# Splitting a fused second MLP into an up phase and a seven-product down phase through DRAM

## The chip, the cores and the metric

The kernel runs on one core of a Trainium2 chip. The metric is the device time of one execution, in microseconds (us). Engines are named as the profile names them: PE (matmuls, with PEld its weight loads), ACT, DVE, POOL, and SP, which here only issues DMAs; POOL issues DMAs from a queue of its own.

## The reference

Three stages follow each other on 8 x 576 = 4608 tokens; everything is float32.

```python
attn: p_packed = sm_attn(p, k, v); x = sm_attn(q, p_packed, p_packed)   # 8 heads of 64, 32 packed queries
mlp 1: x = (silu(x @ w_gate) * (x @ w_val)) @ w_out                     # 512 -> 1536 -> 512
mlp 2: h = x @ w_in; g = h * cos(h); out = g @ w_out                    # 512 -> 2048 -> 512
```

## The kernel before

Every large product is taken in three passes over operands that are split into a high part, rounded for the matmul, and the low rest (`PASSES`): high x high, high x low, low x high. A split costs one ACT copy and one DVE subtraction over the operand (`split`, L103 to L105).

The attention and the up projections of the first MLP run block by block (8 blocks of 576 tokens, `a_up`), to some 430 us. Its down projection (`strassen`, L643 on, called from the loop over `SETS`: four sets of 1024 tokens and one of 512) uses a seven-product scheme: tokens and inner features are halved, the sums of the weight blocks were formed beforehand, those of the data are formed by DVE (`sums1`), each product accumulates in PSUM, and `evict` puts the results together. Its order is `ORDER`; after each product the next one's operands are split (`prep`), and later data is loaded (`load_h`). Results go to DRAM (`x2d`).

Weights arrive packed. `w2_step` does one step of a list (`w2_todo`): decode a block, form sums, split, store to DRAM for later. A pair of blocks takes 7 steps where the seven-product scheme needs it (`w2_pair`: `w1u`, `w2u`), and 2 per block where the weights are used as they are (`w2_put_d`: `w2d`). The steps are placed by hand: at the slots `STEPS` of the attention blocks 1 to 6, at four slots of block 7, and in the first three sets of the first MLP's down projection.

The second MLP runs from 690 us to the end, in one loop over 48 pairs `p` (L1040 on): 6 chunks of 768 tokens (two halves of `TH` = 384) by 8 pairs of feature blocks. Per pair, seven up products (`product`, L989) of six matmuls with 384 columns each go to four PSUM banks; ACT and DVE add them up and form h cos(h) in a four-deep pipeline of tiles of 128 x 384 (`slot`, called by `chain`), which ends with the split that the down projection needs. `step_down` puts down projections between the products: `down` (L1002) takes 128 tokens and four feature blocks, 12 matmuls of 512 columns, and the result is added into `oacc` in SBUF, from where whole rows of 2 KB are stored. Both sorts of weights are loaded again for each chunk, on SP's queue (`load_up`, `load_wd`); x is prepared for the next chunk in between (`load_x2`, `sums_x2`, `split_x2`). All order within an engine is the order of the program text (`manual_schedule`).

## Time and profile before

| what | value |
|---|---|
| median of 3 runs | 1442.2 us (1442.17 to 1444.04) |
| span of the profiled execution | 1440.2 us |
| attention and first up projections | to about 430 us |
| first MLP's down projection | about 430 to 690 us |
| second MLP | 690 us to the end |
| PE busy | 1427.2 us |

The span is the time from the first to the last instruction of one profiled execution; its own device time is not given beside it, so its span is compared with the median, and lies 2.0 us under it. In a profile row, a busy time is the sum over a group, "mean ns" the duration of one instruction, and what follows is the idle time of the engine just before the group's instructions, with what ended it. Instructions of one engine overlap by some tens of nanoseconds at their ends.

### The profile page before, as it was taken

How to read it: one execution, taken by the hardware profiler on the slowest of the kernel's cores; microseconds unless marked ns; L12 is line 12 of the kernel's file. 1: busy time of each engine (PE TensorE's matmuls, PEld its weight loads, DVE VectorE, ACT ScalarE, POOL GpSimd, SP SyncE). 2: the span in 40 equal slices, each digit the busy share in tenths (PEclk: the TensorE clock that was granted, in tenths of full speed). 3: DMA queues.
4: the chain of work that ended last, by engine and by line, in shares of the span. 5: the costliest groups of instructions: out<-in, count | busy, mean ns of one | idle time of the engine just before them, and what ended most of it. 6: DMA issues, size and time to landing. Idle time of an engine off the chain costs nothing.

```text
span 1440.2 us, 24944 instructions
## 1 busy us (share of the span) xinstructions
PE 1427.2 (99%) x9352; PEld 1252.1 (87%) x9352; DVE 1079.8 (75%) x1743; ACT 829.7 (58%) x1462; POOL 126.4 (9%) x232
## 2 busy tenths in 40 slices
PE   8999999999999999999999999999999999999998
PEld 6678888898998878898899999999999999999997
DVE  6769888988948799879867766866776776677564
ACT  5856656656735565554665655646656555555642
POOL 1112222222210111110000000000000000000000
PEclk9999999999999999999999999999999999999999
DMA  8947886795696756570985665685576668556641
GB/s 342 411 165 266 292 328 239 280 335 208 233 410 267 263 204 228 197 249 21 354 286 179 220 221 179 202 294 182 180 242 199 201 213 265 179 178 204 218 142 44
DMA packets 139352, 335.62 MB, mean 233 GB/s; under 512 B 15072, under 2 KB 25312, under 8 KB 137824
## 3 DMA queue, kind: packets, MB, share of 16 engines
q1 hardware_dynamic: 118272, 260.36, 53.5%
q0 software_dynamic: 20096, 71.84, 12.5%
q8 instruction: 74, 1.21, 0.3%
q10 hardware_dynamic: 864, 1.84, 0.3%
q14 instruction: 46, 0.38, 0.1%
HBM read 252.71 MB, written 81.26 MB: 232 GB/s over the span
## 4 chain that ended last, share of the span: by engine, by line
PE 94%; DVE 2%; ACT 1%; DMA 1%; issue 1%; POOL 0%; SPq 0%; ACTq 0%; DVEq 0%
PE acc L1009 27%; PE p L994 23%; PE o L655 16%; PE pg L538 10%; PE pv L538 10%; PE wp L498 3%; PE pv L527 2%; PE pg L527 1%; DMA hr<-h 1%; PE pp L227 1%; PE s L260 1%; PE tp L217 1%; PE s L180 0%; DVE hr L635 0%; DVE g L105 0%
## 5 line engine op out<-in xcount | busy, mean ns | idle before, releaser
L1009 PE MATMUL acc<-wd,g 128*128 128x512 f32 x1728 | 413.8, 389 | 0.0
L994 PE MATMUL p<-xs,up 128*128 128x384 f32 x2016 | 373.2, 337 | 2.9 <-issue 1.6
L1009 PEld LDWEIGHTS acc<-wd,g 128*128 128x128 f32 x1728 | 322.5, 188 | 57.1
L994 PEld LDWEIGHTS p<-xs,up 128*128 128x128 f32 x2016 | 353.7, 188 | 14.7 <-issue 1.9
L655 PE MATMUL o<-g,w 128*128 128x512 f32 (+1 forms) x1260 | 259.3, 368 | 1.0 <-DVE g L105 1.0
L655 PEld LDWEIGHTS o<-g,w 128*128 128x128 f32 x1260 | 219.2, 189 | 40.8 <-DVE g L105 1.7
L972 ACT ACTIVATE t<-c,quarter 128x384 f32<-128x384 f32 x144 | 88.4, 614 | 198.7 <-DVE c L1082 192.9
L538 PEld LDWEIGHTS pg<-a,wp 128*128 128x128 f32 x1008 | 137.8, 188 | 16.1 <-issue 8.2
L104 ACT ACTIVATE g<-hr 128x1024 fp32r<-128x1024 f32 (+1 forms) x105 | 101.5, 976 | 87.1 <-PE o L655 43.9
L538 PE MATMUL pg<-a,wp 128*128 128x288 f32 x1008 | 150.1, 298 | 0.0
L538 PE MATMUL pv<-a,wp 128*128 128x288 f32 x1008 | 150.1, 298 | 0.0
L538 PEld LDWEIGHTS pv<-a,wp 128*128 128x128 f32 x1008 | 137.6, 188 | 7.2 <-DVE h L570 3.3
L105 DVE TENSOR_TENSOR g<-hr,g 128x1024 fp32r<-128x1024 f32 (+1 forms) x105 | 113.4, 1114 | 34.7 <-ACT g L104 34.4
L556 ACT ACTIVATE silu<-pg 128x576 f32<-128x576 f32 x96 | 62.6, 652 | 116.1 <-PE pg L538 107.1
L570 DVE TENSOR_TENSOR h<-silu,pv 128x576 f32<-128x576 f32 x96 | 72.1, 752 | 60.4 <-PE pv L538 25.1
L1077 DVE TENSOR_TENSOR u<-v,p 128x384 f32<-128x384 f32 x48 | 26.6, 553 | 118.2 <-PE p L994 117.9
L982 DVE TENSOR_TENSOR g<-t,g 128x384 fp32r<-128x384 f32 x192 | 105.9, 552 | 8.0 <-ACT g L969 7.8
L974 DVE TENSOR_TENSOR t<-t,k 128x384 f32<-128x384 f32 x192 | 106.0, 552 | 3.5 <-ACT k L978 1.8
L975 ACT ACTIVATE t<-t 128x384 f32<-128x384 f32 x192 | 98.4, 513 | 2.7 <-DVE t L974 2.5
L969 ACT ACTIVATE g<-t 128x384 fp32r<-128x384 f32 x192 | 98.5, 513 | 0.4 <-DVE t L980 0.4
L978 ACT ACTIVATE k<-t 128x384 int32<-128x384 f32 x192 | 98.3, 512 | 0.0
L1023 DVE TENSOR_TENSOR oacc<-oacc,acc 128x512 f32<-128x512 f32 x108 | 73.8, 684 | 32.2 <-PE acc L1009 32.1
(108 smaller groups left out, 1428.7 us busy)
## 6 DMA issues: line engine op xcount, KB each, us to landing
up<-w2u SPq DMA_DIRECT2D x336, 256.0 KB, 3.2
wd<-w2d SPq DMA_DIRECT2D x96, 512.0 KB, 6.2
h<-h POOLq DMA_DIRECT2D x96, 288.0 KB, 4.9
hr<-h SPq DMA_DIRECT2D x48, 512.0 KB, 8.8
raw<-in_w SPq DMA_DIRECT2D x44, 512.0 KB, 4.4
w2u<-w2p POOLq DMA_DIRECT2D x24, 512.0 KB, 3.9
raw<-in_wgv SPq DMA_DIRECT2D x11, 1024.0 KB, 9.9
w<-w1u SPq DMA_DIRECT2D x21, 512.0 KB, 11.6
```

The source lines that it names most:

```text
L104: ACT.activation(out=hi, in_=src, func=AF.Copy)
L105: eng.tensor_tensor(out=lo, in0=src, in1=hi.bitcast(F32), op=ALU.subtract)
L538: PE.matmul(out=p_[:, c, :HS], lhsT=w[:, u, x, o:o + 128], rhs=a2[b][:, u, y, HS * c:HS * c + HS], start=(n == 0), stop=(n == 5),)
L655: PE.matmul(out=acc[:, m, :N], lhsT=wd1[n, fp][:, j, 256 * x + 128 * m:256 * x + 128 * m + 128], rhs=g1[n, fp][:, y, j, :], start=(first a ...
L969: ACT.activation(out=three["g"][:, 0, :], in_=three["t"], func=AF.Copy)
L972: ACT.activation(out=now["t"], in_=now["h"], func=AF.Identity, scale=1.0 / TWO_PI, bias=quarter)
L974: DVE.tensor_tensor(out=one_["t"], in0=one_["t"], in1=one_["k"], op=ALU.subtract)
L975: ACT.activation(out=one_["t"], in_=one_["t"], func=AF.Sin, scale=SIN_SCALE)
L978: ACT.activation(out=now["k"], in_=now["t"], func=AF.Copy)
L982: DVE.tensor_tensor(out=three["g"][:, 1, :], in0=three["t"], in1=three["g"][:, 0, :].bitcast(F32), op=ALU.subtract)
L994: PE.matmul(out=out, lhsT=w[:, u, 128 * k:128 * k + 128], rhs=x[:, v, k, :], start=(first and k == 0 and i == 0), stop=(last and k == 1 an ...
L1009: PE.matmul(out=acc, lhsT=gs[p, a, t][:, x, o:o + 128], rhs=wd[j, f][:, y, :], start=(f == 0 and n == 0), stop=(f == 3 and n == 2),)
```

## The change

The second MLP falls into two phases. In the **up phase** a loop over periods (`period`) works on three pairs at a time: the new pair's products 0, 1 and 2, the old pair's 3, 4, 6 and 5, and h cos(h) of the one before. Partial results are carried into the next product within PSUM: ACT copies one bank into another (`copy(B_, A(new))`, `copy(C(new), B_)`), and the next product accumulates on the copy; `mark` is one matmul that is run on such a bank first. Each tile is now 128 x 2 x 384: ACT takes the phase as an integer, DVE the rest, ACT the sine, DVE the product, and POOL's queue stores g to DRAM (`h2`). The up weights stay in SBUF.

In the **down phase** g comes back chunk by chunk (`load_g`), and the scheme of seven products is used on it too (`down_mm`, `sums2`, `prep2`, `evict2`). The output features lie on the partitions then, so `finish_out` transposes 32 x 32 blocks on DVE and stores pieces of 64 elements. Five of the seven sums of the down weights stay in SBUF; the other two share space and are loaded in turn (`RING`).

The down weights therefore go through `w2_pair` as well: 24 more steps, placed at two more slots in each of the attention blocks 1 to 6, one in block 7, and by `STEPS_D` in the sets. Some small tiles move to another pool. The diff, cut to its core ("..." marks what is left out; the removed loop of the second MLP is in the code above):

```diff
+STEPS_D = ((1, 1, 1, 1, 1, 2, 2), (1, 2, 1, 2, 1, 1, 2), (1, 2, 1, 2, 1, 1, 2), (1, 1, 1, 1, 1, 1, 0), (0,) * 7)
...
+UP_ORDER = (0, 1, 2, 3, 4, 6, 5)
+RING = (4, 2)
...
-STEPS = (1, 2, 3, 5, 6, 7, 8, 9, 11, 14, 16, 17, 18, 20, 21, 22, 23)
+STEPS = (1, 2, 3, 4, 5, 6, 7, 8, 9, 11, 13, 14, 16, 17, 18, 20, 21, 22, 23)
+STEPS_LAST = (0, 2, 4, 6, 8)
+N_EARLY = 6
...
-    w2d = dr.tile([NF2, 128, 2, 512], F32, name="w2d")
+    w2d = dr.tile([NPF, 7, 128, 512], F32, name="w2d")
+    h2 = dr.tile([NF2, 128, NT], F32, name="h2")
...
-    ident = cst.tile([128, 128], F32, name="ident")
-    zero = cst.tile([128, 128], F32, name="zero")
-    pt = [cst.tile([128, NPAIR, NP], F32, name=f"pt{i}") for i in range(2)]
+    ident = pad.tile([128, 128], F32, name="ident")
+    zero = pad.tile([128, 128], F32, name="zero")
+    pt = [pad.tile([128, NPAIR, NP], F32, name=f"pt{i}") for i in range(2)]
...
-    def w2_put_d(i, dst):
-        def act():
-            p = w2_new([128, 2, 512], F32R, "p", "w2p")
-            return split_later(
-                w2_f.pop(i).rearrange("p n c -> p (n c)"), p[:, 0, :], p[:, 1, :],
-                lambda: nc.gpsimd.dma_start(out=dst, in_=p.bitcast(F32)),
-            )
-        return act
...
-    for n in range(0, NF2, 2):
-        i = NW1 + NF2 + n
-        w2_todo += [w2_decode(i), w2_decode(i + 1), w2_put_d(i, w2d[n]), w2_put_d(i + 1, w2d[n + 1])]
+    for n in range(NPF):
+        w2_todo += w2_pair(w2d[n], NW1 + NF2 + 2 * n)
...
-            return lt(shape, dt, "x", name, 7)
+            return lt(shape, dt, "x", name, 16)
...
-        return late["x"].tile([128, 2, 2, TH], F32R, tag="xs", name="xs", bufs=8)
+        return late["x"].tile([128, 2, 2, TH], F32R, tag="xs", name="xs", bufs=9)
...
-                for k in STEPS if b < B - 1 else (0, 2, 4, 6):
+                for k in STEPS if b < B - 1 else STEPS_LAST:
...
-                if s_ in (1, 2) or (s_ == 0 and i > 1):
+                for _ in range(STEPS_D[s_][i]):
                     w2_step()
-                    if s_ and i in (1, 6) or (s_, i) == (1, 3):
-                        w2_step()
-                elif (s_, i) == (3, 0):
+                if (s_, i) == (3, 6):
                     w2_flush()
...
+        def ut(shape, dt, name):
+            return lt(shape, dt, "u", name, 56)
...
+        def load_up(q, n):
+            up[q, n] = ut([128, 2, 256], F32R, "up")
+            SP.dma_start(out=up[q, n].bitcast(F32).rearrange("p x c -> p (x c)"), in_=w2u[q, PIECE[n]])
+        wd = {}
+        wd_first = [(n, f) for n in (0, 4, 6, 1, 3, 5) for f in range(NPF)]
+
+        def load_wd(n, f):
+            wd[n, f] = ut([128, 2, 256], F32R, "wd")
+            SP.dma_start(out=wd[n, f].bitcast(F32).rearrange("p x c -> p (x c)"), in_=w2d[f, PIECE[n]])
...
+        def ac_tile(name):
+            return pu.tile([128, 2, 512], F32, tag="ac", name=name, bufs=3)
+
+        def bd_tiles():
+            return [pu.tile([128, 512], F32, tag=n, name=n)[:, :TH] for n in ("pb", "pd")]
...
-            del up[p, n]
-            load_up(p + 2, n)
+            if q == NPF - 1:
+                xs_of[c][n] = None
+            if c == NCH - 1:
+                del up[q, n]
+                if wd_first:
+                    load_wd(*wd_first.pop(0))
+
+        def mark(out, p):
+            PE.matmul(
+                out=out, lhsT=up[p % NPF, 0][:, 0, :128], rhs=xs_of[p // NPF][0][:, 0, 0, :], start=True, stop=True
+            )
+
+        def store_g(p, t, g):
+            c, q = divmod(p, NPF)
+            r0 = 2 * TH * c + TH * t
+            nc.gpsimd.dma_start(out=h2[2 * q:2 * q + 2, :, r0:r0 + TH].rearrange("f p n -> p f n"), in_=g)
+
+        def phase(out, h_):
+            ACT.activation(out=out.bitcast(I32), in_=h_, func=AF.Copy, scale=1.0 / TWO_PI, bias=0.25)
...
+        def rest(out, h_):
+            DVE.scalar_tensor_tensor(
+                out=out, in0=h_, scalar=1.0 / TWO_PI, in1=out.bitcast(I32), op0=ALU.mult, op1=ALU.subtract
+            )
+
+        def sine(x):
+            ACT.activation(out=x, in_=x, func=AF.Sin, scale=SIN_SCALE, bias=half_pi)
+
+        def times(x, h_):
+            DVE.tensor_tensor(out=x, in0=x, in1=h_, op=ALU.mult)
+
+        def copy(out, in_):
+            ACT.activation(out=out, in_=in_, func=AF.Copy)
+
+        def plus(out, x, y):
+            DVE.tensor_tensor(out=out, in0=x, in1=y, op=ALU.add)
+
+        def xt3(name):
+            return lt([128, 2, TH], F32, "x", name, 16)
...
+        X_SUM = {(3, 1): (0,), (4, 1): (1,), (5, 1): (2,), (5, 2): (3,)}
+        X_NEXT = {(6, 0): (0,), (6, 2): (1,), (7, 1): (2,), (7, 2): (3,)}
+        X_THIS = {(0, 0): (4,), (0, 1): (6,), (0, 2): (5,)}
+        PREP2 = {
+            (LAST, 0): (0, 0), (LAST, 1): (0, 1), (LAST, 2): (0, 2), (LAST + 1, 0): (0, 3),
+            (LAST + 1, 1): (4, 0), (LAST + 1, 2): (4, 1), (LAST + 2, 0): (4, 2), (LAST + 2, 1): (4, 3),
+        }
...
+        def down_mm(i, fps):
+            n = ORDER[i]
+            which = {0: 0, 1: 0, 3: 0, 4: 1, 6: 2, 2: 3, 5: 3}[n]
...
+                    o2 = ac_tile("o2")
+                    acc2[which] = [o2[:, m, :TH] for m in range(2)]
+            acc = acc2[which]
+            for fp in fps:
+                for j in range(2):
+                    for m in range(2):
+                        for q, (x, y) in enumerate(PASSES):
+                            PE.matmul(
+                                out=acc[m], lhsT=wd[n, 2 * fp + j][:, x, 128 * m:128 * m + 128],
+                                rhs=g2[n, fp][:, y, j, :],
+                                start=(first and fp + j + q == 0), stop=(fp, j, q) == (3, 1, 2),
+                                skip_group_check=not first,
+                            )
+                del g2[n, fp]
+            return acc
...
+        def load_g(s_, k, t):
+            if s_ < NCH:
+                r0 = 2 * TH * s_ + TH * t
+                for fp in range(4):
+                    r = raw2[s_, k, t, fp] = xt3("raw2")
+                    f0 = NPF * k + 2 * fp
+                    SP.dma_start(out=r, in_=h2[f0:f0 + 2, :, r0:r0 + TH].rearrange("f p n -> p f n"))
...
+        def prep2(s_, n, fp):
+            if s_ >= NCH:
+                return
+            r = raw2[(s_, *QUAD[n], fp)]
+            g = g2[n, fp] = new_xs()
+            split(r, g[:, 0], g[:, 1])
...
+        def sums2(s_, i):
+            todo = {
+                1: [((0, 1), (0, 1), (0, 0), fp) for fp in range(4)],
+                2: [((1, 1), (1, 1), (0, 1), fp) for fp in range(4)],
+                3: [((0, 0), (1, 1), (0, 0), fp) for fp in range(4)],
+                4: [((1, 0), (1, 0), (1, 1), fp) for fp in (0, 1)],
+                5: [((1, 0), (1, 0), (1, 1), fp) for fp in (2, 3)],
+            }
...
+        def finish_out(s_, a, t, o_):
+            ot = lt([128, TH // 32, 2, 32], F32, "v", "ot", 2)
+            for m in range(2):
+                DVE.transpose(out=ot[:, :, m, :], in_=o_[m])
+            r0 = 2 * TH * s_ + TH * t
+            eng = SP if s_ == NCH - 1 else nc.gpsimd
+            for al in range(4):
+                c0 = 128 * al + 64 * a
+                eng.dma_start(
+                    out=out[r0:r0 + TH, c0:c0 + 64].rearrange("(b r) d -> r b d", r=32),
+                    in_=ot[32 * al:32 * al + 32].rearrange("p b m c -> p b (m c)"),
+                )
+
+        def evict2(s_, n, acc):
+            for m in range(2):
+                if n in (0, 1, 2, 3):
+                    part2[n, m] = ut([128, TH], F32, "part")
+                    copy(part2[n, m], acc[m])
+
+            def pop(k):
...
+            if n == 4:
+                o_ = pop(0)
+                add(o_, o_, acc)
+                finish_out(s_, 0, 0, o_)
+            elif n == 3:
+                w_, c22 = pop(3), pop(2)
+                add(c22, w_, c22)
+                finish_out(s_, 1, 1, c22)
+                add(w_, w_, acc2[2])
+                finish_out(s_, 0, 1, w_)
...
+            if old:
+                copy(old["v"][:, 1], C(old))
...
+                older["p"] = xt3("cp")
+                phase(older["p"], older["ac"][:, :, :TH])
+            if p <= LAST:
+                product(A(new), p, 0, True)
+                if p < 3:
+                    mark(C(new), p)
+                    if p == 0:
+                        mark(B_, p)
+            if old:
+                product(D_, p - 1, 3, True)
+            if p <= LAST:
+                copy(B_, A(new))
...
+                rest(older["p"], older["ac"][:, :, :TH])
+                older["s"] = xt3("cs")
+                phase(older["s"], older["hs"])
+            if old:
+                product(A(old), p - 1, 4, False)
+                old["hs"] = xt3("hs")
+                plus(old["hs"][:, 1], old["v"][:, 1], D_)
+            if older:
+                rest(older["s"], older["hs"])
+                sine(older["p"])
+            x_work(p, 0)
+            if p <= LAST:
+                product(B_, p, 1, False)
+            if old:
+                product(D_, p - 1, 6, False)
...
+                times(older["p"], older["ac"][:, :, :TH])
+                store_g(p - 2, 0, older.pop("p"))
+                del older["ac"]
+            if p <= LAST:
+                copy(C(new), B_)
+                new["v"] = vt()
+                copy(new["v"][:, 0], B_)
+            if older:
+                sine(older["s"])
...
+            if old:
+                product(C(old), p - 1, 5, False)
+                plus(old["hs"][:, 0], old["v"][:, 0], D_)
+            x_work(p, 1)
...
+                times(older["s"], older["hs"])
+                store_g(p - 2, 1, older.pop("s"))
+                del pairs[p - 2]
+            if p <= LAST:
+                product(C(new), p, 2, False)
+            x_work(p, 2)
...
+        for p in range(LAST + 3):
+            if p == LAST - 5:
+                load_g(0, 0, 0)
+            elif p == LAST - 3:
+                load_g(0, 1, 0)
+            period(p)
+        del B_, D_
+        load_g(0, 1, 1)
+        load_g(0, 0, 1)
...
+        for s_ in range(NCH):
+            for i in range(7):
+                n = ORDER[i]
+                acc = down_mm(i, (2, 3) if s_ == i == 0 else range(4))
+                if n in RING:
+                    for f in range(NPF):
+                        del wd[n, f]
+                    if n == RING[1] and s_ + 1 < NCH or n == RING[0]:
+                        for f in range(NPF):
+                            load_wd(RING[1] if n == RING[0] else RING[0], f)
+                if i not in (1, 4):
+                    sums2(s_, i)
+                for fp in range(4):
+                    if s_ + i:
+                        prep2(*nxt2(s_, i), fp)
+                if i in (1, 4):
+                    sums2(s_, i)
+                if i == 4:
+                    load_g(s_ + 1, 0, 0)
+                elif i == 5:
+                    load_g(s_ + 1, 1, 1)
+                    load_g(s_ + 1, 0, 1)
+                elif i == 6:
+                    load_g(s_ + 1, 1, 0)
+                evict2(s_, n, acc)
...
-                moe2_w_out.reshape(NF2, 128, DM),
+                moe2_w_out.reshape(2, NPF, 128, 4, 2, 2, 32).transpose(1, 4, 2, 0, 5, 3, 6).reshape(NF2, 128, 512),
```

## Rows read from the trace of the kernel before

**Rows 1.** The page, part 1: busy us, share of the span, instructions of each engine.
```profile
PE 1427.2 (99%) x9352; PEld 1252.1 (87%) x9352; DVE 1079.8 (75%) x1743; ACT 829.7 (58%) x1462; POOL 126.4 (9%) x232
```

**Rows 2.** Chain that ended last, 849 to 866 us: start us, us, what.
```profile
849.53 3.12 PE p L994 x18
852.65 2.72 PE acc L1009 x12
...
864.99 1.04 PE p L994 x6
```

**Rows 3.** Groups by line and shape, PE: busy us, mean ns, idle before.
```profile
L1009 PE MATMUL acc<-wd,g 128*128 128x512 f32 x1728 | 413.8, 389 | 0.0
L994 PE MATMUL p<-xs,up 128*128 128x384 f32 x2016 | 373.2, 337 | 2.9 <-issue 1.6 <-ACT p L1069 1.3
```

**Rows 4.** Waits of PE, whole span: us in total, times, longest us.
```profile
PE p L994 <- issue: 1.6, 1, 1.6
PE p L994 <- ACT p L1069: 1.3, 1, 1.3
...
PE o L655 <- DVE g L105: 1.0, 1, 1.0
```

**Rows 5.** Windows: us, busy us (count) of PE, PEld, DVE, ACT, POOL; clock, DMA share, GB/s.
```profile
278.00:328.00 50.00, 50.00 (x543) 43.53 (x543) 42.62 (x67) 31.07 (x49) 13.76 (x24) 1.00 0.77 285
...
430.00:487.50 57.50, 57.50 (x256) 47.63 (x255) 48.79 (x49) 31.95 (x39) 4.33 (x8) 1.00 0.76 289
...
603.50:634.40 30.90, 30.90 (x254) 30.68 (x253) 26.51 (x44) 16.69 (x30) 5.41 (x10) 1.00 0.61 214
...
800.00:1000.00 200.00, 200.00 (x1010) 181.69 (x1009) 136.88 (x263) 112.45 (x240) 0.00 (x0) 1.00 0.68 222
```

**Rows 6.** Groups by line and shape, ACT.
```profile
L972 ACT ACTIVATE t<-c,quarter 128x384 f32<-128x384 f32 x144 | 88.4, 614 | 198.7 <-DVE c L1082 192.9 <-DVE c L1093 5.4
...
L978 ACT ACTIVATE k<-t 128x384 int32<-128x384 f32 x192 | 98.3, 512 | 0.0
...
L1069 ACT ACTIVATE p<-p 128x384 f32<-128x384 f32 x48 | 23.5, 489 | 34.1 <-PE p L994 33.6
...
L104 ACT ACTIVATE xs<-xt 128x768 fp32r<-128x768 f32 x24 | 19.3, 837 | 0.0
```

**Rows 7.** Chain that ended last, from 1405 us to the end.
```profile
1409.21 27.21 PE acc L1009 x120
...
1436.45 0.69 DVE oacc L1023
```

**Rows 8.** Groups by line and shape, DVE.
```profile
L974 DVE TENSOR_TENSOR t<-t,k 128x384 f32<-128x384 f32 x192 | 106.0, 552 | 3.5 <-ACT k L978 1.8
...
L129 DVE SCALAR_TENSOR_TENSOR w2f<-w2t,w2f 128x512 uint32<-128x512 uint32 x44 | 30.0, 681 | 0.3 <-ACT w2f L123 0.3
...
L105 DVE TENSOR_TENSOR xs<-xt,xs 128x768 fp32r<-128x768 f32 x24 | 22.7, 955 | 9.7 <-ACT xs L104 9.7
...
L423 DVE TENSOR_TENSOR w2c<-w2f 128x256 f32<-128x256 f32 x28 | 10.5, 417 | 0.0
...
L313 DVE STREAM_TRANSPOSE af<-d 128x576 f32<-128x576 f32 x2 | 1.6, 778 | 0.3 <-POOL d L304 0.2
```

**Rows 9.** DMA issues: time on the issuing engine (POOL, SP), ns.
```profile
L571 POOL DMA_DIRECT2D h<-h x96 | 53.1, 553 | 248.0 <-DVE h L570 232.4 <-DVE rs L209 4.5 <-PE s L260 3.6
...
L606 SPq DMA_DIRECT2D hr<-h x60: 359/427/3065, 389.5 to 629.9; - x60
```

**Rows 10.** The page, parts 3 and 6: DMA queues; issues with us to landing.
```profile
q1 hardware_dynamic: 118272, 260.36, 53.5%
q0 software_dynamic: 20096, 71.84, 12.5%
...
h<-h POOLq DMA_DIRECT2D x96, 288.0 KB, 4.9
...
out<-oacc SPq DMA_DIRECT2D x36, 256.0 KB, 3.8
```

More of the change, by code (lines that the diff above doesn't have):

```diff
@@ L64, in attention_mlp_kernel @@
     cst = ctx.enter_context(tc.tile_pool(name="cst", bufs=1))
[L65 to L66 removed]
+    stage = {n: ExitStack() for n in ("pad", "ups", "att", "gates", "da", "db", "ps", "pu")}
     def pool(n, side=None):
@@ L72, in attention_mlp_kernel @@
     pad = pool("pad", "right")
-    pad.tile([128, 120], F32, name="right_pad")
-    cst.tile([128, 32], F32, name="left_pad")
+    st = stage["pad"].enter_context(tc.tile_pool(name="st", bufs=4, side="right", reuse_waits="tile"))
     att = pool("att")
@@ L927, in attention_mlp_kernel @@
                 evict()
-        for n in ("db", "da", "ps"):
+        for n in ("db", "da"):
             stage[n].close()
-        ps1 = ctx.enter_context(tc.tile_pool(name="ps1", bufs=8, space=bass.MemoryType.PSUM, reuse_waits="tile"))
         late["m"] = ctx.enter_context(tc.tile_pool(name="late", bufs=1, reuse_waits="tile"))
-        def bank(shape, name):
-            return ps1.tile(shape, F32, tag="b", name=name)
-        def tmp(name, dt=F32):
-            return lt([128, TH], dt, "t", name, 16)
@@ L986, in chain @@
-        def chain(p, a, t, h_):
-            gs[p, a, t] = lt([128, 2, TH], F32R, "g", "g2", 16)
-            slot({"h": h_, "g": gs[p, a, t]})
-        def product(out, p, n, x, first, last):
-            w = up[p, n]
+        def ut(shape, dt, name):
+            return lt(shape, dt, "u", name, 56)
+        up = {}
+        def load_up(q, n):
+            up[q, n] = ut([128, 2, 256], F32R, "up")
+            SP.dma_start(out=up[q, n].bitcast(F32).rearrange("p x c -> p (x c)"), in_=w2u[q, PIECE[n]])
@@ new lines, in attention_mlp_kernel, with vt @@
+        wd = {}
[3 more added lines that the diff above has]
+            SP.dma_start(out=wd[n, f].bitcast(F32).rearrange("p x c -> p (x c)"), in_=w2d[f, PIECE[n]])
+        def vt():
+            return lt([128, 2, TH], F32, "v", "v", 2)
+        for q in range(3):
+            for n in UP_ORDER:
+                load_up(q, n)
+        xs_of = {0: x_now}
+        pairs = {}
+        stage["ps"].close()
@@ new lines, in attention_mlp_kernel, with product @@
+        pu = stage["pu"].enter_context(
+            tc.tile_pool(name="pu", bufs=1, space=bass.MemoryType.PSUM, reuse_waits="tile")
+        )
[3 more added lines that the diff above has]
+            return [pu.tile([128, 512], F32, tag=n, name=n)[:, :TH] for n in ("pb", "pd")]
+        B_, D_ = bd_tiles()
+        LAST = NCH * NPF - 1
+        def product(out, p, n, first):
+            c, q = divmod(p, NPF)
+            w, x = up[q, n], xs_of[c][n]
@@ L1103, in attention_mlp_kernel @@
-        while d_next < len(downs):
-            step_down(NP_ALL + 2)
-            run(post)
+                        start=(first and k == 0 and i == 0), stop=(k == 1 and i == 2), skip_group_check=not first,
+                    )
+            if q == NPF - 1:
[8 more added lines that the diff above has]
+            )
@@ L1108 @@
+        stage["pu"].close()
 _OUT = ((NT, DM), "float32")
```

213 lines of the change are left out of this document (63 added, 150 removed).

## The prediction

> **What bounds the kernel now.** I read the busy times first: TensorE (PE) is busy 99% of the span, DVE 75%, ACT 58%, POOL 9% [rows 1]. Since a busy PE need not be a PE at its peak, I then read the chain of waits in a plain stretch of the second MLP [rows 2]: it consists of matmuls alone, 18 up products in 3.12 us and 12 down products in 2.72 us, without a gap. So 384 columns cost 3.12/18 = 0.1736 us and 512 columns 2.72/12 = 0.2267 us. One loop step of 42 up and 36 down matmuls is 42 x 0.1736 + 36 x 0.2267 = 15.45 us; the chain repeats after 864.99 - 849.53 = 15.46 us. The second MLP, from 690.0 to 1436.4 us, holds 2016 up and 1728 down matmuls [rows 3]: 350.0 + 391.7 = 741.7 us of 746.4. The waits of PE [rows 4] name nearly all of the rest, 1.6 + 1.3 us, both at the stage's start. The granted clock is 1.00 in all stages [rows 5], the upper level (2.4 GHz), so it gives nothing back. In this part of the kernel a matmul taken away is time taken away, as long as nobody else becomes late.
>
> **The sum** is made against the profiled execution's span, 1440.2 us; the median of the runs, 1442.2, lies 2.0 above it, and I carry these 2.0 over. Of the measured difference about 0.2% (3 us) can be told from none.
>
> 1. Down projection on PE. Removed: 1728 x 0.2267 = 391.7. Added, per chunk of 768 tokens: seven products x 8 feature blocks x 2 output halves x 3 passes = 336 matmuls of 384 columns, 2016 in six chunks, at 0.1736: 350.0. These have the shape of the up products, with new weights in each as there, so the price needs no bound. **-41.7.**
>
> 2. Four marking matmuls: +0.7. The first period has no older pair between its products, so PE waits for two seeding copies, each 0.49 by the copy out of PSUM [rows 6] and a handoff (0.02 us at the end [rows 7]): 1.0 to 1.2. The old start lost 1.3 to such a copy [rows 4]. Net 0; the 1.6 there, late weights, I keep.
>
> 3. Up phase, 48 periods of 42 x 0.1736 = 7.29 us of PE. ACT's new form is not in the trace: a copy PSUM to PSUM, a scaled conversion to int32 of 768 elements, a sine with a bias tile. Nearest rows: 0.49 for a copy of 384, 0.84 for 768, 0.10 more for a bias tile (614 against 512) [rows 6]. Per period 4 x 0.49 + 4 x 0.84 + 2 x 0.10 = 5.5. DVE: four passes over 768 at 0.95 (the scalar form costs 0.68 at 512, on the line between 0.55 at 384 and 0.95 at 768) and two over 384 at 0.55: 4.9 [rows 8]. Preparing the next chunk adds 7 splits and, on DVE, 4 sums per 8 periods: ACT 6.3, DVE 6.2 on average; the first period of a chunk, with three splits, 8.0 and 7.8. That is 0.7 too much once, followed by periods with none. Deadlines, in us from the period's start: the copy that seeds B follows C's copy and the phase on ACT's queue, ready at 0.6 + 0.84 + 0.49 = 1.9, needed at 3.1 (three products of 1.04 lie before); the one that seeds C is queued behind a phase, a sine and at most a split, ready near 5.0, needed at 6.3; DVE frees D at 2.9, needed at 4.2; and frees the old pair's banks at 5 to 6, needed at 7.3. Each has a microsecond of cover. I take 0; bounds 0 and 0.5 per period (24), as a chain of two unseen PSUM operations could be half a microsecond late. Nothing can be gained: PE runs gapless in rows 2. If the cover went, ACT would be late next, then everything behind it on its queue. POOL gets 96 stores here and 80 of the output's later, at 0.55 each [rows 9]; it issues nothing now in this stage [rows 5].
>
> 4. Change of phase. PE keeps 24 matmuls of product 0 and 48 each of products 4 and 6 (4.2 + 8.3 + 8.3 us) after the last up product. In that time the last pair's chain ends (two phases, rest, sine, product, store: some 5 us), its store lands (4.9), quadrant (0,1) is loaded into its buffers (taken as long as a store, 4.9 [rows 10]), and DVE does eight sums, two adds, two transposes and a split (10.8). One after the other that is 25.6 against 20.8. Between 0 and 6, taken **+2**: nearer the low end, since only the last two of the eight buffers are that late.
>
> 5. Down phase, 58.3 us of PE per chunk. DVE: 28 splits at 0.95, 16 sums at 0.95, 8 adds at 0.55, 8 transposes of 384 at 0.55 (0.78 for 576 is on the same line) [rows 8] = 50.7, 87%; ACT 28 x 0.84 + 8 x 0.49 = 27.4. The worst product has four adds and four transposes, then four splits: 8.2 of 8.3, and only the first split is due at once. On SP's queue the reload of the ring weights waits for product 2 to end, and the next chunk's loads wait behind it; due a product and a half later (12 us), are 2 + 1.5 MB, at the queue's 338 GB/s (rival (b)) 10 us. Taken 0, bounds 0 and 3 per chunk.
>
> 6. Weights. The 16 blocks of the down weights now go through the seven-block scheme, 7 steps per pair instead of 4 per pair: 24 steps more. A pair costs DVE 4 x 0.68 to decode, 3 x 0.68 and 5 x 0.42 for splits and sums = 6.9 [rows 8], about 0.98 per step. Thirteen go into the attention stage (DVE 43 of 50 us there [rows 5]: two more per block still fit; +0.5, bounds 0 and 3), four more into the first 512-token set, one into the third, six into the 256-token set, whose window is 30.9 us with DVE at 26.5 [rows 5]: 26.5 + 5.9 = 32.4. **+1.5**, bounds 0 and 4 with what the denser stores delay: one wait for a split is already there [rows 4].
>
> 7. Tail. Before: one add and one store, 3.8 us after the last matmul [rows 7]. After: two adds and two transposes (1.7 behind the last matmul), four store issues on SP at 0.43 [rows 9], and a landing of 3.1 to 7, the median of `out` being 3.8 [rows 10]: 1.7 + 1.3 + 4 = 7.0. **+3**, bounds 2 and 7.
>
> Sum: -41.7 + 0.7 + 2 + 0.5 + 1.5 + 3 = -34: span 1406, time **1408**.
>
> **Rivals.**
> (a) The up phase runs at the pace of its PSUM copies. For: an up product already waited for such a copy behind a full ACT queue [rows 4]; ACT is at 86% of a period. Against: that wait came once. Price: 0.2 to 0.5 in each of 48 periods, 10 to 24 us: 1418 to 1432.
> (b) Slower: the output's scattered stores fill the DMA engines in the down phase. Each row of a tile is now written as pieces of 256 bytes, 6144 per chunk, where the old store wrote 2 KB. No row shows the price of such a piece. Below, by bytes alone: the 16 engines move 338 GB/s when busy (260.36 MB in 53.5% of the span [rows 10]), 21 GB/s each, so 256 bytes take 12 ns. Above, as dear as a mean packet of that queue: 0.535 x 1440.2 x 16 / 118272 = 104 ns, 40 us per chunk on 16 engines. The rest of a chunk's traffic, 6.3 MB of g and 4.2 MB of weights, takes 31 us at 338 GB/s. At the upper price 71 us stand against 58.3: 6 x 12.7 = 76 us late, time 1484. It decides at (58.3 - 31) x 16 / 6144 = 71 ns, and outweighs the gain (34 + 3 us, 6.2 per chunk) from 87 ns. I take 49 ns, an estimate: the two queues have packets of 2201 bytes at 104 ns and of 3575 bytes at 0.125 x 1440.2 x 16 / 20096 = 143 ns [rows 10], and the line through both gives 49 at 256 bytes. The chunk then needs 31 + 19 = 50 us and nothing shows; 71 is near enough to leave the rival a tenth. The Trainium skill (DMA: Bandwidth & Descriptors, Specifications) wants at least 512 B per piece and says that below it the engine reads, modifies and writes. By that rule, read as twice the bytes, a piece would cost 24 ns and this rival would fall away altogether; no row here shows it.
> (c) The waits of points 4 to 7 come at their upper bounds: above the values taken 4, 5 and 4 us, 1421; 1432 with 11 of the 18 that point 5 could cost. DVE at 87% speaks for it; against it, that the seven products of the first MLP run at 85% DVE [rows 5] with one wait of 1.0 [rows 4].
> (d) The change doesn't do what it says: the columns that PE streams fall by an eighth in the down projection by the loops themselves, so only the rate could differ, and the up products show it. 1%.
>
> **Chances.** Forecast 0.65, (a) 0.13, (b) 0.10, (c) 0.11, (d) 0.01. The likeliest case spans -41.7 + 0.7 + 2 (tail's least) = -39 to -27: 1403 to 1415. The range 1402 to 1430 adds most of (a) and (c) and leaves out (b). Faster 0.87 (forecast, nearly all of (a) and (c)), slower 0.10, same 0.03.
>
> **What the changed profile would show.** Right: 4036 or so matmuls of 384 columns in the second MLP at 0.174 each, PE without idle groups, a period of 7.3 us, a chunk of 58.4 us, ACT and DVE at most 86% busy in the up phase, DVE near 85% in the down phase. Wrong by (a): idle time of PE released by ACT's copies, a period of 7.5 to 7.8. By (b): DMA share near 9 tenths throughout the down phase and waits for the loads of g. By (c): waits of PE for splits at the phase change, at chunk starts, in the 256-token set, or a tail of 10 us.

## The result and the profile after

The changed kernel takes 1421.45 us (median of 4 runs, 1418.5 to 1423.24) against 1443.12 for the kernel before (4 runs beside it): a ratio of 0.9842, 95% interval 0.9822 to 0.9861, so 1.4 to 1.8% faster. Forecast were 1408 and a range of 1402 to 1430. The sign and the range hold; in the spans, 10.5 of the 34 us that were forecast did not come. The profiled execution of the changed kernel took 1418.5 us with a span of 1416.7, and lies 3 us under its median.

Since the stages follow each other without overlap on PE, the difference can be cut at three marks in the trace: the first matmul of the first MLP's down projection, the first of the second MLP, and the end of the last matmul.

| us | starts down projection | its length | second MLP | after the last matmul | span |
|---|---|---|---|---|---|
| before | 430.04 | 260.17 | 746.2 | 3.8 | 1440.2 |
| after | 435.91 | 265.85 | 708.7 | 6.3 | 1416.7 |
| difference | +5.9 | +5.7 | -37.5 | +2.5 | -23.5 |
| forecast | +0.5 | +1.5 | -39.0 | +3 | -34 |

So the rebuilt stage did what was forecast of it to within 1.5 us, and the tail to within 0.5. The loss, 11.6 us against 2.0 forecast, lies in two stages in which hardly a line of the computation was changed. First what came true. The chain that ended last, in a stretch of the up phase (start us, us, what), answers to [rows 2]:

```profile
833.01 3.12 PE ac L956 x18
836.13 1.04 PE pd L956 x6
837.17 1.04 PE ac L956 x6
838.21 1.04 PE pb L956 x6
839.25 1.04 PE pd L956 x6
840.29 3.12 PE ac L956 x18
```

A period is 840.29 - 833.01 = 7.28 us of matmuls without a gap (7.29 forecast). The windows below (columns as in [rows 5]) are the start of the up phase, the change of phase, and one chunk of the down phase:

```profile
690.00:720.00 30.00, 26.62 (x127) 23.64 (x126) 15.75 (x21) 12.09 (x21) 3.24 (x6) 0.94 0.69 254
1040.00:1100.00 60.00, 57.26 (x330) 56.68 (x328) 51.33 (x63) 35.76 (x52) 8.22 (x12) 1.00 0.83 294
1160.83:1219.07 58.24, 58.24 (x337) 58.24 (x337) 46.22 (x61) 24.95 (x37) 9.88 (x16) 1.00 0.62 208
```

The chunk takes 58.24 us (58.3 forecast), PE is busy all of it, DVE 79%, the DMA engines 62%. What the down phase writes in such a chunk is the queue q0 (packets, MB, share of 16 engines) in that window:

```profile
q0 software_dynamic: 768, 1.57, 9.7%
```

6144 pieces of 256 bytes cost 0.097 x 58.24 x 16 / 6144 = 14.7 ns of one engine each, close to the 12 ns of the price by bytes. The line through the two queues' mean packets, 49 ns, was three times too dear, and the mean is far below the 71 ns from which rival (b) decides. The rule of the Trainium skill that the prediction quoted (DMA: Bandwidth & Descriptors, Specifications) would give an estimate of 24 ns, read as twice the bytes; this trace shows less than that too.

The waits of PE in the whole span (us in total, times, longest us), beside [rows 4]:

```profile
PE pv L532 <- DVE h L564: 2.8, 5, 1.4
PE ac L956 <- DMA up<-w2u: 2.1, 1, 2.1
PE o L1040 <- DVE xs L109: 2.1, 1, 2.1
PE o L649 <- DVE g L109: 1.4, 2, 0.8
...
PE o L649 <- ACT g L108: 0.7, 1, 0.7
PE o L1040 <- ACT xs L108: 0.6, 1, 0.6
```

and, in the same view of 595 to 720 us, the two for the seeding copies:

```profile
PE pb L956 <- ACT pb L992: 0.6, 1, 0.6
PE ac L956 <- ACT ac L992: 0.6, 1, 0.6
```

Three groups: attention (`pv`), the 256-token set and the one after it (`o` L649), and the starts of the two phases (`ac`, `pb`, `o` L1040). The change of phase runs as the prediction wrote it out; the chain that ended last there:

```profile
1069.74 5.12 DMA h<-cs
1074.86 0.02 issue
1074.88 3.66 DMA raw<-h
...
1078.64 0.96 DVE raw L1079
1079.59 0.93 DVE part L995 x2
1080.52 0.95 DVE ot L1084 x2
1081.47 3.45 DVE raw L1079 x4
1084.92 0.88 DVE xs L109
1085.80 0.04 issue
1085.84 4.27 PE o L1040 x23
```

The last pair's store lands, its buffers take the fourth quadrant, and DVE finishes sums, adds, transposes and a split: 2.1 + 0.6 = 2.7 us of waiting against +2 forecast.

What did not come true is not a wait. In the first MLP's down projection the waits above sum to 2.1 us, 1.1 more than before, yet the stage is 5.7 us longer. The matmuls of that stage in the same stretch of 25.5 us (count, duration in ns min/median/max, first and last start), before and after:

```profile
L655 PE MATMUL o<-g,w x114: 389/389/389, 444.8 to 470.4; 128*128 128x512 f32 x114
```
```profile
L649 PE MATMUL o<-g,w x110: 392/397/401, 444.8 to 470.3; 128*128 128x512 f32 x110
```

From start to start a matmul of 512 columns takes (470.4 - 444.8) / 113 = 226.5 ns before and 25.5 / 109 = 233.9 ns after, with PE busy throughout and the granted clock at 1.00, the upper level. Taken from the starts of all 1260 matmuls in the trace, a product of 36 takes 8.16 us before; after, the products 4, 6, 1 and 2 take 8.43 and the other three 8.16. Sixteen of them at +0.27 us are 4.3 us. The 256-token set, whose matmuls have 256 columns, shows no such loss (last section). What these four share is the pool in which their weights lie (`gates`); the weights of products 0, 3 and 5 lie in `da` and `db`.

### The profile page after: what moved, and what is told of

The parts are those of the page before. It is cut to its first block, busy times and chain, and to the rows that moved or that the text cites. A ratio compares the mean times of both kernels' runs of the same rounds, so it can differ in the third digit from the quotient of the medians.

```text
span 1416.7 us, 25273 instructions
## 1 busy us (share of the span) xinstructions
PE 1393.8 (98%) x9644; PEld 1279.2 (90%) x9644; DVE 1130.8 (80%) x1515; ACT 827.9 (58%) x1226; POOL 257.9 (18%) x424
## 4 chain that ended last, share of the span: by engine, by line
PE 74%; issue 13%; DVE 5%; POOL 3%; DMA 3%; ACT 2%; SPq 0%; POOLq 0%; DVEq 0%; ACTq 0%
PE o L649 17%; PE o L1040 16%; PE pv L532 7%; PE pg L532 7%; PE ac L956 7%; PE pb L1040 4%; PE pd L1040 3%; PE pd L956 3%; PE wp L492 2%; POOL h L975 2%; PE pb L956 2%; PE pv L521 2%; PE pg L521 1%; DMA hr<-h 1%; PE pp L231 1%
## 5 line engine op out<-in xcount | busy, mean ns | idle before, releaser
L649 PE MATMUL o<-g,w 128*128 128x512 f32 (+1 forms) x1260 | 263.9, 371 | 2.1 <-DVE g L109 1.4
L649 PEld LDWEIGHTS o<-g,w 128*128 128x128 f32 x1260 | 219.4, 188 | 46.3 <-DVE g L109 1.9
L1040 PE MATMUL o<-xs,wd 128*128 128x384 f32 x1440 | 252.4, 336 | 2.7 <-DVE xs L109 2.1
L1040 PEld LDWEIGHTS o<-xs,wd 128*128 128x128 f32 x1440 | 249.8, 188 | 3.3 <-DVE xs L109 2.4
L956 PE MATMUL ac<-xs,up 128*128 128x384 f32 x1152 | 217.0, 337 | 2.8 <-DMA up<-w2u 2.1
L956 PEld LDWEIGHTS ac<-xs,up 128*128 128x128 f32 x1152 | 201.8, 189 | 3.5 <-DMA up<-w2u 2.5
L109 DVE TENSOR_TENSOR xs<-raw,xs 128x768 fp32r<-128x768 f32 x168 | 149.6, 948 | 33.7 <-ACT xs L108 33.7
L108 ACT ACTIVATE xs<-raw 128x768 fp32r<-128x768 f32 x168 | 132.0, 843 | 73.3 <-DVE raw L1079 71.1
L956 PE MATMUL pd<-xs,up 128*128 128x384 f32 x576 | 115.8, 337 | 0.0
L564 DVE TENSOR_TENSOR h<-silu,pv 128x576 f32<-128x576 f32 x96 | 72.1, 751 | 52.3 <-PE pv L532 16.9
L956 PEld LDWEIGHTS pd<-xs,up 128*128 128x128 f32 x576 | 101.4, 189 | 0.2
L565 POOL DMA_DIRECT2D h<-h x96 | 53.2, 555 | 243.8 <-DVE h L564 221.8
L1079 DVE TENSOR_TENSOR raw<-raw,raw 128x768 f32<-128x768 f32 x96 | 85.4, 947 | 3.0 <-DMA raw<-h 3.0
```

What stands on the lines that cost most here:

```text
L108: ACT.activation(out=hi, in_=src, func=AF.Copy)
L109: eng.tensor_tensor(out=lo, in0=src, in1=hi.bitcast(F32), op=ALU.subtract)
L564: DVE.tensor_tensor(out=h_, in0=s_, in1=pv[:, :, :HS], op=ALU.mult)
L565: nc.gpsimd.dma_start(out=h1[f, :, S * b:S * b + S], in_=h_.rearrange("p c n -> p (c n)"))
L649: PE.matmul(out=acc[:, m, :N], lhsT=wd1[n, fp][:, j, 256 * x + 128 * m:256 * x + 128 * m + 128], rhs=g1[n, fp][:, y, j, :], start=(first a ...
L956: PE.matmul(out=out, lhsT=w[:, u, 128 * k:128 * k + 128], rhs=x[:, v, k, :], start=(first and k == 0 and i == 0), stop=(k == 1 and i == 2) ...
```

## The experiments

Two theories stood at first. The **steps** theory: the 24 weight steps added beside the attention and the sets are what was lost. The **copies** rival: the periods of the up phase run at the pace of the seeding copies, so that the second MLP hides a loss. A third, the **address** theory, came out of the first run: the `gates` weights are read more slowly because the pool moved.

**1. The weight steps taken out.** The down weights go to DRAM block by block, decoded and split, in place of the sums of the seven-product scheme; the sums of the down weights are left out, their place in DRAM is filled with plain blocks, and all slots are those of the kernel before. All else, the matmuls and the bytes stored, is as after the change.

```diff
-    for n in range(NPF):
-        w2_todo += w2_pair(w2d[n], NW1 + NF2 + 2 * n)
+    for n in range(NPF):
+        i, d_ = NW1 + NF2 + 2 * n, w2d[n]
+        w2_todo += [
+            w2_decode(i), w2_decode(i + 1), w2_plain(i, d_[0:2], d_[2:3]), w2_plain(i + 1, d_[3:5], d_[5:7]),
+        ]
...
-STEPS = (1, 2, 3, 4, 5, 6, 7, 8, 9, 11, 13, 14, 16, 17, 18, 20, 21, 22, 23)
+STEPS = (1, 2, 3, 5, 6, 7, 8, 9, 11, 14, 16, 17, 18, 20, 21, 22, 23)
```

> The changed kernel, but the down weights take 4 steps per pair as before the change, at the old slots: their sums are left out, and each stored piece is a split block as it was decoded (the same bytes are stored). The output is then not the reference's. Theory (the 24 extra steps cost the 11.6 us that stand between 0 and the second MLP): the first MLP's down projection starts at 430 instead of 435.9, the second MLP at 690 to 691 instead of 701.8, ratio to the kernel before 0.976 to 0.978. Rival (something else in the changed kernel slows the first 700 us: the moved pools, the larger stores): both starts stay within 2 us of 435.9 and 701.8, ratio 0.983 to 0.985.

Measured: 1413.56 us, ratio 0.9803 (0.9786 to 0.9819). The down projection starts at 430.94, so the 13 steps beside the attention cost 435.91 - 430.94 = 5.0 us. Between 100 us and that start PE has no named wait any more, as before the change; with the 13 steps the named ones sum to 3.2 us of the 5.0 (2.8 for `h`, 0.4 for `E`). But the stage itself still takes 264.15 us, 4.0 more than before, and its four products still take 8.43 us without a step added anywhere. So the steps theory holds for the attention alone; of the sets' 5.7 us it explains 1.7. Some 0.9 us of the attention's lateness is left.

**2. The sums of the weight steps on POOL.** The same work, off the loaded engine.

```diff
-            DVE.tensor_tensor(out=o_, in0=x, in1=y, op=op)
+            nc.gpsimd.tensor_tensor(out=o_, in0=x, in1=y, op=op)
```

> The changed kernel with all its steps, but the four sums of each weight pair (256 elements each) run on POOL instead of DVE, for all 22 pairs. Theory (the extra steps cost time because DVE gets behind): 22 x 4 x 0.42 = 37 us leave DVE, more than the 24 x 0.98 = 23 that the change added, so the attention stage ends by 431, the 256-token set takes 31 us again and the ratio falls to 0.975 to 0.978. Rival (the steps cost time on ACT's queue, where a step's copies and decodes stand ahead of the silu that frees PE's banks): the attention stage still ends at 435 or later, ratio 0.982 to 0.985. A third case: POOL takes longer per sum (its operation on 576 elements took 1.16 us) and holds up the stores behind it, ratio above 0.985.

Measured: 1432.39 us, ratio 0.9933 (0.9917 to 0.9949): by the ratios (0.9933 - 0.9842) x 1442 = 13 us slower than the changed kernel. The down projection starts at 444.01, 8.1 later. Its waits in the attention, and two softmax rows of DVE (min/median/max):

```profile
PE pg L532 <- DVE wp L117: 5.0, 3, 2.1
PE pv L532 <- DVE h L564: 2.8, 5, 1.4
...
L292 DVE TENSOR_TENSOR d<-d,mx x6: 1357/1358/2618, 115.9 to 373.4; 128x1152 f32<-128x1152 f32 x6
...
L308 DVE TENSOR_TENSOR d<-d,sm x6: 1357/1358/2899, 124.6 to 384.7; 128x1152 f32<-128x1152 f32 x6
```

A sum costs 813 to 1051 ns on POOL against 417 on DVE, and the waits for `h` stay as they were. Two-input operations on DVE that took 1359 ns at most after the change now take up to 2.6 and 2.9 us. The Trainium skill says that the two engines share one pair of SBUF ports, locked for a whole instruction (SBUF — State Buffer, SBUF: two separate sides). The two maxima agree with it in kind; the 1.3 and 1.5 us that they add are more than one sum.

**3. Each seeding copy made twice.** The direct test of rival (a).

```diff
                 copy(B_, A(new))
+                copy(B_, A(new))
...
                 copy(C(new), B_)
+                copy(C(new), B_)
```

> The changed kernel with each of the two seeding copies in PSUM issued twice in a row, so that ACT has 2 x 0.48 us more per period and both hand-offs to PE come 0.48 us later or more. Theory (each hand-off has about a microsecond of cover): the period stays at 7.28 us, PE shows no waits in the up phase except in its first periods, total within 3 us of the changed kernel. Rival (the up phase runs close to the pace of its PSUM copies): 0.3 to 0.5 us per period, 14 to 24 us in all, waits of PE for ACT's copies.

Measured: 1425.43 us, ratio 0.9886 (0.9866 to 0.9906). From the first up matmul to the first down matmul it takes 357.49 us against 353.69: 3.8 us for 96 more copies of 0.48, where the rival expected 14 to 24. The busy times over the same 202 us, after and with the double copies:

```profile
833.00:1035.00 202.00, 202.00 (x1168) 201.86 (x1166) 156.42 (x201) 150.08 (x243) 40.12 (x56) 1.00 0.44 166
```
```profile
833.00:1035.00 202.00, 201.27 (x1150) 198.44 (x1149) 156.28 (x198) 172.82 (x295) 39.37 (x55) 1.00 0.43 162
```

ACT goes from 74 to 86% and PE loses 0.7 us of 202. Taken from the starts of the up matmuls, the loss lies at one place: from the second chunk on, the first period of a chunk takes 7.96 us and the second 7.60, the others 7.28 as without the extra copies. That is 1.0 us in each of five chunks, at the period with three splits that the prediction had named as 0.7 too much for ACT. PE's waits from 760 to 1040 us, where the unchanged kernel has none:

```profile
PE pb L956 <- ACT pb L992: 1.0, 5, 0.2
```

So the copies had a copy's length of cover in most periods, and less at the chunk starts. The five chunks cost 5.0 us; the difference of 3.8 is smaller because the changed kernel's profiled execution lost 1.7 us to a lower clock in its first periods, which this one did not (last section). Rival (a) falls: without the extra copies no period is longer than 7.30 after the first one and before the change of phase.

**4. Order and queues.** On top of run 2: the buffers for the first up weights taken in another order, and the last chunk's stores put on SP's and ACT's queue in turn.

```diff
+        early = [(q, n) for q in range(3) for n in UP_ORDER]
+        for q, n in early[:6] + early[-4:] + early[6:-4]:
+            up[q, n] = ut([128, 2, 256], F32R, "up")
...
-            eng = SP if s_ == NCH - 1 else nc.gpsimd
             for al in range(4):
+                eng = nc.gpsimd if s_ < NCH - 1 else (SP, ACT)[al % 2]
```

> The kernel with the sums on POOL, and two edits in the second MLP: the first up weights are put into buffers that are free earlier (four of them lay over an operand of the first MLP's last product), and the last chunk's output stores are issued from SP and ACT in turn instead of SP alone. Theory: the 2.1 us wait of PE for an up weight goes, and some 1 us of the tail's four issues; ratio 0.002 below that of the run with the sums on POOL alone. Rival (the wait is then taken over by the bank or by a split that is late next, and the tail is set by the landing): no difference beyond 0.001.

Measured: 1429.97 us, ratio 0.9914 (0.9899 to 0.9929). The 0.0019 under run 2 is what the theory forecast, but the two intervals overlap, and it is not the theory's wait that went. The span ends 5.9 us after the last matmul (6.3 in run 2), a gain of 0.4. The wait for the first up weights stays, 2.5 us against 2.4: the order of the buffers is not what makes them late, and what does was not tried further.

**5 to 8. The address.** The diff of the change also removes two idle tiles that held other pools at their place, and puts small ones at the right end of SBUF:

```diff
-    pad.tile([128, 120], F32, name="right_pad")
-    cst.tile([128, 32], F32, name="left_pad")
```

By the two programs' tile addresses, `gates` began at byte 179,712 of a partition before, a multiple of 512, and begins at 173,920 after, 32 past a multiple of 64. `da` and `db` begin 256 past a multiple of 512 after the change. Four kernels move the pools and nothing else.

*Run 5, the changed kernel with idle tiles of 352 and 256 bytes per partition:*

```diff
     pad = pool("pad", "right")
+    pad.tile([128, 88], F32, name="right_pad")
+    cst.tile([128, 64], F32, name="left_pad")
```

> The changed kernel with two idle tiles put back: 352 bytes per partition at the right end of SBUF and 256 at the left, so that the pools gates and ups (the first MLP's weights) begin at a multiple of 512 bytes again, as in the kernel before; after the change they begin 32 bytes past a multiple of 64. Nothing that is computed, and no order, differs. Theory A (the address sets the pace of the matmuls that read those weights): the 16 products of 36 matmuls that take 8.43 us after the change go back to 8.16 us, the first MLP's down stage goes from 265.9 to 261.6 us, perhaps another us in the attention stage, whose fused weights lie in ups; 1416 to 1418 us in all. Theory B (the slow products come from the instruction streams beside them): 8.43 us as before, 1421 us.

*Run 6, the kernel before with its right-hand idle tile 32 bytes shorter:*

```diff
-    pad.tile([128, 120], F32, name="right_pad")
+    pad.tile([128, 112], F32, name="right_pad")
```

> The kernel before with its right-hand idle tile cut from 480 to 448 bytes, so that gates and ups alone begin 32 bytes past a multiple of 64; nothing else differs. Theory A (address): 16 products of its down stage go from 8.16 to 8.43 us, the stage from 260.2 to 264.5 us, the time from 1443 to 1447 to 1449 us. Theory B (instruction streams): 1443 us, 8.16 us.

*Run 7, the changed kernel with an idle tile of 32 bytes at the right end (`pad.tile([128, 8], F32, ...)`), and run 8, made last of all, with one of 224 bytes (`pad.tile([128, 56], F32, ...)`):*

> The changed kernel with one idle tile of 32 bytes at the right end alone: gates and ups then begin at a multiple of 64 that is no multiple of 128 or 512 (gates at 173,888 = 64 x 2717). If it is the multiple of 64 that counts, the products take 8.16 us and the time is as that of the version with both idle tiles, 1416 to 1418 us; if the wider multiple counts, 8.43 us or something between, and 1419 to 1421 us.

> The changed kernel with one idle tile of 224 bytes at the right end: gates then begins at 173,696, a multiple of 128 but not of 256. With 32 past a multiple of 64 the products took 8.43 us, at an odd multiple of 64 8.40 us, at a multiple of 512 8.16 us; the pools da and db, at 256 past a multiple of 512, take 8.16 us. If a multiple of 128 is enough, 8.16 us here, a down stage of some 261.5 us and 1416 to 1419 us; if 256 is needed, 8.3 to 8.4 us, 265 us and 1420 to 1423 us.

Measured, in the order of the runs, the row shown above of before and after; the last two rows are runs 7 and 8:

```profile
L651 PE MATMUL o<-g,w x114: 389/389/389, 444.8 to 470.4; 128*128 128x512 f32 x114
```
```profile
L655 PE MATMUL o<-g,w x111: 395/396/396, 444.6 to 470.3; 128*128 128x512 f32 x111
```
```profile
L650 PE MATMUL o<-g,w x111: 393/393/398, 444.7 to 470.4; 128*128 128x512 f32 x111
```
```profile
L650 PE MATMUL o<-g,w x111: 390/393/404, 444.7 to 470.3; 128*128 128x512 f32 x111
```

| `gates` begins | ns from start to start | product of 36, us | down projection, us | median, ratio to before |
|---|---|---|---|---|
| at a multiple of 512 (run 5) | 226.5 | 8.16 | 261.5 | 1417.71, 0.9827 (0.9812 to 0.9842) |
| 32 past one of 64 (run 6, before's code) | 233.6 | 8.40 | 262.4 | 1444.74, 1.0016 (1.0006 to 1.0025) |
| at an odd multiple of 64 (run 7) | 233.6 | 8.40 | 265.5 | 1422.99, 0.9865 (0.9845 to 0.9885) |
| at an odd multiple of 128 (run 8) | 232.7 | 8.37 | 264.9 | 1421.63, 0.9853 (0.9816 to 0.9889) |

Run 5 gives the stage 4.4 us back (265.85 to 261.47), and its four products are at 8.16 again. In the whole time only some 2 us of it show, (0.9842 - 0.9827) x 1442, and the two intervals overlap: the second MLP of its profiled execution was 3.9 us longer (last section). Run 6 takes the same away from the kernel before by 32 bytes of an idle tile: its products go from 8.16 to 8.40 and its time rises by 2.8 us, less than the 16 x 0.24 = 3.8, since the wait of 1.0 us in that stage [rows 4] is not in run 6's. Both show the address theory, run 6 in the whole time too. A multiple of 64 or 128 is not enough. The pools `da` and `db`, at 256 past a multiple of 512, run at 8.16, so a multiple of 256 seems to be; `gates` itself was not put at one. The attention stage gains nothing from run 5 (the down projection starts at 436.59), though its fused weights moved too, as they lie in `ups`. How the address slows a matmul is not shown; only that it does.

**9. Two steps per block on other slots.** Run 5 with the steps of slots 4 and 13 on 0 and 19.

```diff
-STEPS = (1, 2, 3, 4, 5, 6, 7, 8, 9, 11, 13, 14, 16, 17, 18, 20, 21, 22, 23)
+STEPS = (0, 1, 2, 3, 5, 6, 7, 8, 9, 11, 14, 16, 17, 18, 19, 20, 21, 22, 23)
```

> The version with both idle tiles, and the two weight steps per block that the change put on slots 4 and 13 of the attention stage put on slots 0 and 19 instead, which hold no other softmax work; as many steps as after the change. Theory P (the two places cost, since they hold up softmax work or h that the matmuls wait for): the first MLP's down stage begins at 431 to 433 us instead of 435.9, and the time is 2 to 4 us under the version with idle tiles alone. Theory Q (the amount of work on VectorE and ScalarE costs, wherever it stands): 435 to 436 us, and no gain.

Measured: 1416.55 us, ratio 0.9817 (0.9802 to 0.9831). The down projection starts at 434.22 instead of 436.59. The waits of `pv` for `h` are gone, smaller ones have come:

```profile
PE pg L534 <- DVE wp L119: 1.0, 3, 0.5
PE wp L494 <- DVE h L566: 0.4, 1, 0.4
PE pv L534 <- DVE wp L119: 0.3, 2, 0.2
```

The place is worth 2.4 us at this start, half of what the 13 steps cost, which lies between the two expectations. The median is 1.2 us under run 5's, less than the 2 to 4 of theory P, and the intervals overlap.

**10 and 11. A version that takes up what was found.** Run 9 with four more moves, each in a stage of its own; run 11 moves two steps per block once more.

```diff
-STEPS_D = ((1, 1, 1, 1, 1, 2, 2), (1, 2, 1, 2, 1, 1, 2), (1, 2, 1, 2, 1, 1, 2), (1, 1, 1, 1, 1, 1, 0), (0,) * 7)
+STEPS_D = ((1, 2, 1, 2, 1, 2, 2), (2, 2, 1, 2, 1, 2, 2), (2, 2, 1, 2, 1, 2, 2), (0,) * 7, (0,) * 7)
...
+            elif p == LAST + 2:
+                load_g(0, 1, 1)
             period(p)
...
-        load_g(0, 1, 1)
         load_g(0, 0, 1)
```

> The version with idle tiles and slots 0 and 19, with four more moves, each in a stage of its own: the six weight steps of the 256-token set and its flush put into the sets before (35 steps as before); the last eviction of the first MLP ahead of six of the seven input splits; the third group of reloaded hidden tiles loaded one period earlier; the last chunk's stores alternately on SP's and ScalarE's queue. Theory: each wait that the trace shows at these places goes, 0.9 us in the 256-token set, 2 us at the last set's start, up to 1.4 us at the first up products, 3.3 us at the first down products with 1.7 us of half clock behind them, 1 us in the tail: 1406 to 1411 us. Rival: a wait that goes is given back at the next, since VectorE is 90 per cent busy in the sets and SP's queue holds the loads in order: 1413 to 1417 us.

> The same as the version with the four moves, with two weight steps per attention block moved again, from slots 18 and 22, which follow the fused weights' second splits, to slots 12 and 15. If the fused weights' splits that wait behind those steps are what is left of the attention stage's lateness, the first MLP's down stage begins 1 to 3 us earlier than 434.2 us; if the amount of work is, it stays at 434 us, or is later since slots 12 and 15 hold softmax work.

Measured: run 10 takes 1413.83 us, ratio 0.9797 (0.9782 to 0.9813), level with run 1, which leaves the sums out, while run 10 has them. By the ratios it is (0.9842 - 0.9797) x 1442 = 6.5 us under the changed kernel, and the two intervals do not overlap. The down projection takes 260.9 us, 0.7 less than in run 9: the waits in and after the 256-token set are gone, but one of 1.4 us has come between 500 and 600 us, where the steps now stand. The tail is 5.9, 0.4 less. But the waits at the first up and down products did not go:

```profile
PE ac L960 <- DMA up<-w2u: 2.6, 1, 2.6
PE o L1044 <- DVE xs L111: 2.1, 1, 2.1
...
PE o L1044 <- ACT xs L110: 0.9, 1, 0.9
```

Loading the third quadrant earlier is no help where the fourth one's buffers are the late ones. So the theory fell at these two places, and the median lies in the rival's 1413 to 1417.

Run 11 takes 1416.06 us, ratio 0.9808 (0.9792 to 0.9824), and starts the down projection at 438.36, 3.5 us later than run 10: `PE pv` waits for `h` again, 5.5 us over ten times. Slots 12 and 15 hold softmax work. Both runs have as many steps; the slot decides more than the count.

## Why the prediction was right, and where it was wrong

The mechanism was right: matmuls taken away were time taken away. The wrong terms of the sum lie outside the stage that was rebuilt.

Point 1 (-41.7) held: period and chunk came out at 7.28 and 58.24 us. Point 2: the wait that was kept at 1.6 measured 2.1, the two for copies 1.2 as forecast. (That the old 1.6 were late weights was a reading; the row in [rows 4] names no releaser. After the change the row names the load.) Point 3, taken at 0, held; run 3 shows the cover that it claimed, except in the first two periods of a chunk, where the extra copies no longer fit. Point 4 (+2) measured 2.7, by the chain that was written out. Point 5 (0) held: no wait of PE in the chunk shown, DVE at 79% (87% forecast). Point 7 (+3) measured 2.5.

Point 6 failed in one half. The sets cost 1.7 by run 1 (+1.5 forecast). The attention was costed at +0.5, bounds 0 and 3, because two more steps per block "still fit" into DVE's idle 7 us of 50; it measured 5.0, beyond the bound. Fitting by the mean busy time was the error. A step at a given slot stands in DVE's and ACT's queues ahead of `h` or of a softmax operation, and PE waits for that one; runs 9 and 11 each move two steps per block, at the same count, and get -2.4 and +3.5 us.

The other failed step has no number in the prediction at all: the small tiles that move to another pool, and the idle tiles that go, were not priced. They cost 4.4 us by run 5. No row of the trace before compares two addresses, so no bound could have come from it; but it should have been asked what an idle tile is there for.

These two account for 4.5 + 4.4 of the 10.5 us by which the profiled execution missed the sum. Some 0.9 us of the attention's lateness stays in run 1 too and was not settled; the second MLP's +1.5 is no more than its waits (0.5 and 0.7 above the values taken) and the granted clock, below, can make. Of the rivals, (a) is refuted by run 3, (b) by the 14.7 ns, (d) by the pace of the periods and chunks. The time lies at the lower end of (c), and half of the way there is (c)'s: the attention's bound was reached and passed, while the waits came only 0.7 above the value taken at point 4, 0.2 at the sets, and none at point 5. The other half, the address, no rival had: that the range held although it was missing is luck, since the range had been widened for (a) and (c).

## What to carry to other kernels

Before a pool or an idle tile is moved, note where each weight tile begins, and compare the time of one matmul per pool afterwards: PE stays 100% busy and only the pace from start to start tells. Work that is added beside a bound engine is priced by the slot at which it stands in its engine's queue and by who waits behind it, not by the engine's mean busy share.

## What the hardware showed that was not expected

Weights that begin off a multiple of 256 bytes cost, at the three sorts of address tried here, 6 to 7 ns per matmul of 512 columns (226.5 to 232.7 or more). It is not so at every length. In the 256-token set the products 4, 6, 1 and 2 run with 256 columns, here before and in run 6, whose `gates` lies 32 bytes off:

```profile
L655 PE MATMUL o<-g,w x142: 283/283/283, 607.3 to 624.2; 128*128 128x256 f32 x142
```
```profile
L655 PE MATMUL o<-g,w x142: 277/280/285, 609.1 to 625.8; 128*128 128x256 f32 x142
```

From start to start that is 16.9 / 141 = 119.9 ns before and 16.7 / 141 = 118.4 with the 32 bytes: a little faster, not slower. The moving tiles of the up phase (`xs`) begin off such a multiple both before and after, and their matmuls show no loss: 3.12 / 18 = 173.3 ns for 384 columns lies on the line through the 119.9 for 256 and the 226.5 for 512 (173.2). That comparison is only argued; `xs` was not moved.

The granted clock fell after waits of some 2 us at the start of a phase. After the change it is 0.94 over 690 to 720 us (shown above), a start with waits of 2.1 and twice 0.6; within that, a window of 708.9 to 712.3 us has 0.50, the lower level (1.2 GHz). Before, with waits of 1.6 and 1.3 [rows 4], it is 1.00 in the same window:

```profile
690.00:720.00 30.00, 27.10 (x149) 25.43 (x148) 23.94 (x47) 20.06 (x45) 1.08 (x2) 1.00 0.97 360
```

The sum of the waits alone does not decide: run 3 has 1.1, 1.1 and 1.0 there and keeps 1.00. In run 5 the clock falls at the change of phase too, with waits of 2.1 and 1.9 where the profiled execution above had 2.1 and 0.6 and kept 1.00:

```profile
690.00:720.00 30.00, 26.81 (x132) 24.45 (x131) 15.03 (x20) 13.47 (x24) 3.47 (x7) 0.94 0.83 305
1040.00:1100.00 60.00, 56.00 (x306) 55.42 (x306) 48.08 (x59) 33.14 (x48) 8.22 (x12) 0.94 0.76 264
```

On top of the waits, 0.5 x 3.4 = 1.7 us of full clock are lost in the first window and about 0.06 x 60 = 3.6 in the second. Run 5's second MLP takes 712.6 us against 708.7 with the same code, and of the changed kernel's four runs the shortest, 1418.5 us, has a mean granted clock of 0.998, the longest, 1423.24, one of 0.995. This would explain why the profiled execution lies under the median, and why the median gained less than the spans say; no run here removed the waits, so it is not shown.
